# Three opening sums moved from between the parts of the last chunk to behind the chunk before it

## The chip, the core and the metric

The kernel runs on one core of one Trainium2 chip. The metric is the device time of one execution in microseconds. A time given with a place ("at 399.35") is counted from the first instruction of the profiled execution.

## The reference

Two stages follow each other. The first is causal attention with a decay bias, for 8 batches, 8 heads, 576 tokens and head size 64:

```python
cum = np.cumsum(np.maximum(s, 0.0), axis=-1)
bias = -(cum[:, :, :, None] - cum[:, :, None, :])
scores = np.where(causal, -1e9, scale * q @ k.T + np.minimum(bias, 0.0))
x = softmax(scores) @ v          # laid out as (8, 576, 512)
```

The second mixes the tokens in the frequency domain, keeps 64 modes, and adds a channel product:

```python
X = np.fft.rfft(x, axis=1)[:, :64]
Y = X @ (w_r + 1j * w_i)         # one 512x512 complex matrix for each mode
u = x + np.fft.irfft(Y, n=576)   # 8 x 576 x 512
out = u + np.maximum(u @ w_ch, 0.0)
```

The weights of the modes are 64 x 512 x 512, real and imaginary, in float32; they are the largest input.

## The kernel before

The work has four groups of channels (`g`, two heads each), eight batches, and eight chunks (`c`) of eight modes each. During attention the weights of the modes stream in as bfloat16, in the order group, chunk, real then imaginary, all through GpSimd's DMA queue (`load`, L243). The products of a chunk (`modes`, L478) run as soon as its weights are on chip; for the first three groups they are added up in `y_acc`. The last group of channels (`NG - 1`) ends each chunk: its product plus `y_acc` is the chunk's spectrum `yb` (name `y_sb`, DVE, L502).

From there the kernel computes u = x + G y and z = u w_ch = x w_ch + G (y w_ch), where G is the inverse transform. The order of all instructions is written by hand; each engine goes through its own in that order. For each chunk, `y_transposed` (L701, copy on ACT L703) and `y_times_wch` (L709, copy on DVE L713) make `vb`, which is the chunk's y w_ch. Both y and y w_ch go to `yv`, with 16 rows for each chunk: for the first chunks by copies, for the later ones by DMAs on SP (`spread`, L513).

The output is worked off in 18 pairs of token tiles. PSUM holds a `u` tile (two banks) and `z` tiles for a pair. Four functions add to them on TensorE: `add_x` (L803, x itself, starts u), `add_y` (L773, rows of yv; here the first 96, which are chunks 0 to 5), `add_last` (L784, one single chunk, straight from `y_sb` or `v_sb` without yv), and `x_times_wch` (L681), which opens z for pairs 0 and 1 earlier on. Pair 0 is two full token tiles (2 matmuls for each sum); pair 1 is four half tiles that run two at a time (4 matmuls).

Chunk seven is the last of the stream, and its imaginary half comes in two halves with DMAs of their own. So `modes` takes its 16 products in four parts: parts 0 and 1 need the real weights, part 2 the first half of the imaginary ones, part 3 the second. Through `meanwhile` the kernel can put other matmuls in front of a part:

```python
for x in range(4):
    ri, y = divmod(x, 2)
    if meanwhile and x in meanwhile:
        meanwhile[x]()
    for z in range(4):
        ...
```

Before the change part 2 has in front of it the sums of z (`first_z` of pairs 0 and 1) over chunks 0 to 5 and chunk 6, and part 3 those of u of pair 0 (`first_u`): x, chunks 0 to 5, chunk 6.

After chunk seven comes its own transposition (L904), its share in u of pair 0 (L784), its product with w_ch (L911, copies L914), its share in z of pairs 0 and 1 (L784), and then a hand-written list of steps that finishes one pair after the other: relu on ACT (L826), sums on DVE (L848, L850) and GpSimd (L832), output DMAs on SP (L854, L857).

Of the kernel before, what the change touches and what calls it, by code (L numbers as in the profile page):

```python
# [18 lines left out]
def kernel(  # L19
# [20 lines left out]
    NG = DM // P  # L40
# [6 lines left out]
    NCK = NM // MC  # L47
# [160 lines left out]
    def ring_of(k):  # L208
        if k < NE:
            return None  # L210
        return int(k < LW2 and (k - NE) % (WA + WB) >= WA)
# [42 lines left out]
    for n in range(N):  # L254
# [4 lines left out]
        while nt < min(w // 2, len(wq)):  # L259
            i = ring_of(nt)  # L260
# [209 lines left out]
    def modes(g, c, meanwhile=None):  # L470


        ps = auxpool.tile([P, DM], FP32, name="yp", tag="aux")
        cols = xs[g % 2].rearrange("p q k h r b m -> p q k (h r b) m")

        def product(ri, q_, cg):
            k0 = HP if ri == 1 and c == 0 and cg == 0 else 0
            nc.tensor.matmul(  # L478
                ps[32 * cg : 32 * cg + 32, :],
                cols[k0:, q_, 1 - ri, :, c * MC // 2 + cg],  # L480
                wt[(g, c, ri)][cg // 2][k0:, 2 * (cg % 2) + q_, :],
                start=(ri == 0 and q_ == 0), stop=(ri == 1 and q_ == 1),
                tile_position=(k0, 32 * cg), skip_group_check=True,
# [7 lines that stand above are left out]
                if meanwhile:  # L491
                    product(ri, z // 2, 2 * y + z % 2)
                else:
                    product(ri, y, z)
        if g == 0:
            nc.vector.tensor_copy(out=y_acc[:, c, :], in_=ps)
        elif g < NG - 1:
            nc.vector.tensor_tensor(out=y_acc[:, c, :], in0=ps, in1=y_acc[:, c, :], op=ALU.add)  # L498
        else:
            yb = spool.tile([P, DM], FP16, name="y_sb", tag="y")  # L500
            for cols in halves if c == NCK - 1 else [slice(0, DM)]:
                nc.vector.tensor_tensor(  # L502
                    out=yb[:, cols], in0=ps[:, cols], in1=y_acc[:, c, cols], op=ALU.add
                )
            if c >= NCK - 2:
                spread(c, 0, yb)
            return yb
# [3 lines left out]
    def spread(c, which, rows):  # L511

        nc.sync.dma_start(out=yv[16 * c : 16 * c + 16, :, which, :], in_=rows)  # L513
# [68 lines left out]
    with tc.tile_pool(name="sc_psum", bufs=2, space=PSUM) as scpool, \  # L582
# [8 lines left out]
        for n in range(N):  # L591
# [21 lines left out]
            i = first_pairs[n - N + len(first_pairs)] if n >= N - len(first_pairs) else None  # L613
# [42 lines left out]
    def parts(b, T):  # L656

        if T < NF:
            return [(slice(0, P), b, ident16h)]
        return [(slice(NL * i, NL * i + NL), b + i, ident16h[:NL, :NL]) for i in range(2)]  # L660
# [37 lines left out]
    def y_transposed(yb, c=NCK):  # L698
        ps = auxpool.tile([P, DT, P], FP16, name="yt_ps", tag="aux")
        for dt in range(DT):  # L700
            nc.tensor.transpose(ps[:, dt, :], yb[:, bass.ts(dt, P)], ident16h)  # L701
        yt = yt_first[:, :, c % NY, :] if c < NCK - 2 else spool.tile([P, DT, P], FP16, name="yt_sb", tag="yt")
        nc.scalar.copy(out=yt, in_=ps)  # L703
        return yt

    def y_times_wch(c, yt):
        vp = auxpool.tile([P, DM], FP32, name="v_ps", tag="aux")
        for dt in range(DT):
            nc.tensor.matmul(  # L709
                vp, yt[:, dt, :], wch_sb[:, dt, :], start=(dt == 0), stop=(dt == DT - 1)  # L710
            )
        vb = spool.tile([P, DM], FP16, name="v_sb", tag="v")
        nc.vector.tensor_copy(out=vb, in_=vp)  # L713
        spread(c, 1, vb)
        return vb
# [50 lines left out]
    GK = P - 2 * MC * NX  # L766

    def add_y(dst, i, which, rows=slice(0, P), start=False, xx=(0, 1)):

        for x in xx:  # L770
            b, T = pairs[i][x]
            for r, bb, _ in parts(b, T):
                nc.tensor.matmul(  # L773
                    dst[x][r, :], G_sb[rows, bass.ds(T * P, r.stop - r.start)],
                    yv[rows, bb, which, :], start=start, stop=True, skip_group_check=True,
                    tile_position=(0, r.start),
                )

    def add_last(dst, i, yb, cols=slice(0, DM), c=NX - 1, xx=(0, 1)):

        for x in xx:
            b, T = pairs[i][x]
            for r, bb, _ in parts(b, T):
                nc.tensor.matmul(  # L784
                    dst[x][r, cols], Gx_sb[:, c, bass.ts(T, P)] if T < NF else Gt_sb[:, bb, c], yb[:, cols],
                    start=False, stop=True, skip_group_check=True, tile_position=(0, r.start),
                )
# [3 lines left out]
    def start_u(i):  # L791
        if upools[i % 2] is None:
            (xt, aux)[i % 2].close()
            upools[i % 2] = ctx.enter_context(
                tc.tile_pool(name=f"u_psum{i % 2}", bufs=1, space=PSUM, side=("left", "right")[i % 2])
            )
        us[i] = upools[i % 2].tile([P, 2, DM], FP32, name="u_ps", tag="u")

    def add_x(i):
        start_u(i)  # L800
        for x, (b, T) in enumerate(pairs[i]):
            for r, bb, ident in parts(b, T):
                nc.tensor.matmul(  # L803
                    us[i][r, x, :].rearrange("p (g d) -> p g d", d=P), ident,
                    x_all[: r.stop - r.start, :, bb, T, :],
                    start=True, stop=False, skip_group_check=True, tile_position=(0, r.start),
                )

    def u_of(i):
        return [us[i][:, x, :] for x in range(2)]  # L810
# [48 lines left out]
    def z_of(i):  # L859
        return [zs[i, x] for x in range(2)]  # L860

    for c in range(NCK - 2):
        yb = modes(NG - 1, c)
# [17 lines left out]
    assert not order_z and not ahead  # L881
    c = NCK - 2
    yb6 = modes(NG - 1, c)
    yt = y_transposed(yb6)
    vb6 = y_times_wch(c, yt)


    def first_u():
        add_x(0)
        add_y(u_of(0), 0, 0, slice(0, GK))  # L890
        add_last(u_of(0), 0, yb6, c=0)

    def first_z(i):
        add_y(z_of(i), i, 1, slice(0, GK))
        add_last(z_of(i), i, vb6, c=0)

    yb = modes(NG - 1, NCK - 1, {2: lambda: (first_z(0), first_z(1)), 3: first_u})

    yt = spool.tile([P, DT, P], FP16, name="yt_sb", tag="yt")
    for x in range(2):  # L900
# [51 lines left out]
    for step in (  # L952
# [8 lines left out]
        i = int(step[1:].rstrip("ab"))  # L961
# [34 lines left out]
```

## Time and profile before

| | |
|---|---|
| median of 3 runs | 441.92 us (440.32 to 442.31) |
| the profiled execution | 442.11 us, of which the span from first to last instruction is 440.3 us |
| PE (TensorE matmuls) busy | 340.8 us, 77% |
| DVE, ACT, POOL busy | 252.5, 226.0 and 171.7 us |
| mean granted TensorE clock | 0.925 |
| DMA | 93.30 MB, mean 212 GB/s |
| chain that ended last | DMA 53%, PE 25%, DVE 15% |

PE is the matmul side of TensorE; DVE, ACT and POOL are VectorE, ScalarE and GpSimd; SP is the queue that issues the output and `yv` DMAs. "Busy" counts modelled ends of pipelined matmuls, so a busy PE need not be at its peak. "PEclk" is the share of the full TensorE clock that was granted: 1.00 or 0.50. The chain of waits is followed back from the last instruction, at each step to what released it. In a timeline row the first number is the start, the second how long the group of instructions took.

### The profile page before, as it was taken

What the parts mean: (1) busy time and instruction counts of PE and PEld (TensorE: products, weight loads), DVE (VectorE), ACT (ScalarE), POOL (GpSimd) and SP (SyncE); (2) the same over time, 40 slices, a digit from 0 to 9 for tenths busy, and PEclk for the clock granted to TensorE, in tenths of its full rate; (3) what the DMA queues carried; (4) which work ended last, traced back from release to release, by engine and by line L of the source; (5) the groups of instructions that cost most, each with busy time, mean ns of one, the idle gap of its engine ahead of it and who ended that gap; (6) DMA issues with size and microseconds to landing.
All of it is one profiled execution on the core that took longest, in us unless ns stands there. A gap on an engine that the chain in (4) does not pass through costs nothing.

```text
span 440.3 us, 10592 instructions
## 1 busy us (share of the span) xinstructions
PE 340.8 (77%) x4409; PEld 203.7 (46%) x4409; DVE 252.5 (57%) x574; ACT 226.0 (51%) x421; POOL 171.7 (39%) x257
## 2 busy tenths in 40 slices
PE   1588999899695977973939458899987797778995
PEld 1365666465463644641616125556554345432341
DVE  7667776677573555752715315766655344450795
ACT  1387878267463634860727024766651334330794
POOL 6555454424353444323444343433322212310293
PEclk9999999999988888995968767999999989996999
DMA  9999999999999999999999999999999999996498
GB/s 179 207 206 206 204 206 208 207 209 207 207 205 207 210 207 210 207 209 208 205 209 208 209 208 209 207 210 206 210 211 212 212 211 211 203 218 121 155 381 347
DMA packets 69063, 93.30 MB, mean 212 GB/s; under 512 B 25932, under 2 KB 27592, under 8 KB 69016
## 3 DMA queue, kind: packets, MB, share of 16 engines
q0 software_dynamic: 61424, 81.28, 104.6%
q1 hardware_dynamic: 7592, 11.36, 7.2%
q8 instruction: 34, 0.56, 0.5%
q14 instruction: 13, 0.11, 0.1%
HBM read 163.58 MB, written 9.51 MB: 393 GB/s over the span
## 4 chain that ended last, share of the span: by engine, by line
DMA 53%; PE 25%; DVE 15%; issue 3%; POOL 2%; ACT 1%; DVEq 0%; POOLq 0%
DMA w_sb<-in_moe_w_i_dram 21%; DMA w_sb<-in_moe_w_r_dram 17%; DMA qk<-in_k_dram 8%; DMA qk<-in_q_dram 5%; PE sc_ps L397 3%; DVE xs L468 3%; DVE qt L359 3%; PE z_ps L681 3%; PE yp L478 3%; DVE x_all L443 2%; PE av_ps L433 2%; PE sc_ps L391 2%; PE tr_ps L355 2%; DVE xt L553 2%; PE z_ps L773 2%
## 5 line engine op out<-in xcount | busy, mean ns | idle before, releaser
L405 ACT ACTIVATE p_sb<-sc_ps,cumt_sb 128x576 f16<-128x576 f32 (+1 forms) x256 | 141.9, 636 | 21.8 <-PE sc_ps L397 21.4
L397 PE MATMUL sc_ps<-qt,kt 128*128 128x512 bf16 (+2 forms) x384 | 76.8, 312 | 6.9 <-ACT kt L359 6.1
L243 POOL DMA_DIRECT2D v<-in_v_dram x72 | 51.4, 714 | 60.6 <-DMA w_sb<-in_moe_w_i_dram 12.8
L243 POOL DMA_DIRECT2D w_sb<-in_moe_w_i_dram x62 | 38.5, 623 | 89.2 <-DMA w_sb<-in_moe_w_i_dram 28.3
L359 DVE COPY qt<-tr_ps 64x576 bf16<-64x576 bf16 x64 | 47.8, 747 | 41.5 <-PE tr_ps L355 41.5
L478 PE MATMUL yp<-w_sb,xs 128*32 128x512 bf16 (+1 forms) x480 | 42.2, 431 | 29.1 <-DMA w_sb<-in_moe_w_i_dram 25.4
L355 PE MATMUL tr_ps<-ident,qk 64*64 64x64 bf16 x1152 | 34.3, 205 | 33.8 <-DMA qk<-in_k_dram 16.0
L243 POOL DMA_DIRECT2D w_sb<-in_moe_w_r_dram x60 | 37.4, 624 | 53.0 <-DMA w_sb<-in_moe_w_r_dram 33.3
L397 PEld LDWEIGHTS <-kt 128*128 128x128 bf16 x384 | 38.3, 105 | 34.5 <-ACT kt L359 12.8
L391 PE MATMUL sc_ps<-negm,ident 128*128 128x256 bf16 x256 | 53.5, 293 | 0.1
L355 PEld LDWEIGHTS <-qk 64*64 64x64 bf16 x1152 | 26.4, 117 | 51.7 <-DVE kt L359 20.3
L376 ACT ACTIVATE p<-sc_ps,cumt 128x64 f16<-128x64 f32 x32 | 10.1, 314 | 73.8 <-PE sc_ps L372 73.6
L433 PE MATMUL av_ps<-v,p_sb 128*128 128x65 f16 x1024 | 44.2, 197 | 1.8 <-DVE x_all L443 0.6
L359 ACT COPY kt<-tr_ps 64x576 bf16<-64x576 bf16 x32 | 22.8, 714 | 40.8 <-DVE qt L359 40.1
L433 PEld LDWEIGHTS <-p_sb 128*128 128x128 f16 x1024 | 37.4, 100 | 9.6 <-DVE x_all L443 5.4
L468 DVE CAST xs<-ft_ps 64x128 bf16<-64x128 f32 x128 | 36.7, 287 | 7.3 <-PE ft_ps L458 5.7
L478 PEld LDWEIGHTS <-xs 128*32 128x32 bf16 (+1 forms) x512 | 17.8, 146 | 46.0 <-DMA w_sb<-in_moe_w_i_dram 24.6
L438 DVE TENSOR_REDUCE den<-av_ps 128x5 f32<-128x10 f32 x64 | 10.8, 169 | 48.3 <-PE av_ps L433 47.3
L443 DVE TENSOR_TENSOR x_all<-av_ps,rcp 128x320 f16<-128x320 f32 x64 | 31.5, 492 | 2.2
L498 DVE TENSOR_TENSOR y_acc<-yp,y_acc 128x512 f32<-128x512 f32 x16 | 11.1, 692 | 29.2 <-PE yp L478 28.5
L539 ACT COPY z<-z_ps 128x512 f32<-128x512 f32 x22 | 12.9, 586 | 26.9 <-PE z_ps L571 14.2
L458 PE MATMUL ft_ps<-Ff_sb,x_all 128*64 128x192 f16 (+1 forms) x320 | 24.4, 266 | 1.0 <-DVE x_all L443 1.0
(107 smaller groups left out, 439.4 us busy)
## 6 DMA issues: line engine op xcount, KB each, us to landing
w_sb<-in_moe_w_r_dram POOLq DMA_DIRECT2D x60, 512.0 KB, 13.6
w_sb<-in_moe_w_i_dram POOLq DMA_DIRECT2D x55, 512.0 KB, 13.2
out_dram<-r_w SPq DMA_DIRECT2D x16, 512.0 KB
v<-in_v_dram POOLq DMA_DIRECT2D x72, 64.0 KB, 11.1
qk<-in_q_dram POOLq DMA_DIRECT2D x15, 288.0 KB, 12.0
qk<-in_k_dram POOLq DMA_DIRECT2D x15, 288.0 KB, 13.2
x_all<-in_moe_w_r_dram POOLq DMA_DIRECT2D x4, 512.0 KB, 8.4
w_sb<-in_moe_w_i_dram POOLq DMA_DIRECT2D x3, 384.0 KB, 12.7
```

The costliest lines, as they stand in the source:

```text
L243: nc.gpsimd.dma_start(out=dst, in_=src)
L355: nc.tensor.transpose(ps[rows, r, :], src[rows, r, :], ident16[rows, rows])
L359: copy(out=to[:, :, :, half * RH : half * RH + RH], in_=ps[HP * i : HP * i + HP].rearrange("d r (h p) -> d h p r", h=2),)
L391: nc.tensor.matmul(ps[:, bass.ds(w * S, W)], ident16, negm[:, bass.ts(r, W)], start=True, stop=False, skip_group_check=True,)
L397: nc.tensor.matmul(ps[:, c0 : c0 + i1 - i0], keys[:, w, r, :], qh[:, i0:i1], start=False, stop=True, skip_group_check=True,)
L405: nc.scalar.activation(out=pt[:, poff[x] : poff[x] + S - w * W], in_=ps[:, w * S : (w + 1) * S - w * W], func=ACTF.Exp, bias=cumt_sb[:, x, ...
L433: nc.tensor.matmul(ps[:, I, r : r + NCH], lhsT, rhs, start=(i == 0), stop=(i == len(todo) - 1), skip_group_check=True,)
L443: nc.vector.tensor_tensor(out=x_all[:, g, b, :, D * h : D * h + D], in0=ps[:, :, 1 : NCH], in1=rcp.unsqueeze(2).to_broadcast([P, NT, D]), ...
L458: nc.tensor.matmul(ps[HP * q_ : HP * q_ + HP].rearrange("p h f -> p (h f)"), x_all[:nT, g, b, T, q_::2], Ff_sb[:nT, T, :], start=(T == 0), ...
L468: nc.vector.tensor_copy(out=xs[g % 2][HP * h : HP * h + HP, q_, :, h, :, b, :], in_=a)
L478: nc.tensor.matmul(ps[32 * cg : 32 * cg + 32, :], cols[k0:, q_, 1 - ri, :, c * MC // 2 + cg], wt[(g, c, ri)][cg // 2][k0:, 2 * (cg % 2) + ...
L681: nc.tensor.matmul(zs[i, x], xts[i][:, x, dt, :], wch_sb[:, dt, :], start=(dt == 0), stop=(last and dt == DT - 1), skip_group_check=True,)
```

## The change

The sums of u of pair 0 over x, chunks 0 to 5 and chunk 6 go behind chunk six: `add_x` in front of chunk six's transposition, the other two between it and `y_times_wch`. The sums of z of pairs 0 and 1 over chunks 0 to 5 go behind `y_times_wch` of chunk six. The sums of z over chunk six stay in front of part 2 of chunk seven; part 3 has nothing in front of it any more.

```diff
     c = NCK - 2
     yb6 = modes(NG - 1, c)
+    add_x(0)
     yt = y_transposed(yb6)
+    add_y(u_of(0), 0, 0, slice(0, GK))
+    add_last(u_of(0), 0, yb6, c=0)
     vb6 = y_times_wch(c, yt)
-
-
-    def first_u():
-        add_x(0)
-        add_y(u_of(0), 0, 0, slice(0, GK))
-        add_last(u_of(0), 0, yb6, c=0)
+    add_y(z_of(0), 0, 1, slice(0, GK))
+    add_y(z_of(1), 1, 1, slice(0, GK))
 
     def first_z(i):
-        add_y(z_of(i), i, 1, slice(0, GK))
         add_last(z_of(i), i, vb6, c=0)
 
-    yb = modes(NG - 1, NCK - 1, {2: lambda: (first_z(0), first_z(1)), 3: first_u})
+    yb = modes(NG - 1, NCK - 1, {2: lambda: (first_z(0), first_z(1))})
```

## The prediction

> **What bounds the kernel now.** I read the slices of the span first, then the chain that ended last, then the PE timeline around the edit, then the landings of the last weights, and last the granted clock in stretches cut where it changes.
>
> From the page, the granted clock and the DMA share by slice:
>
> ```profile
> PEclk9999999999988888995968767999999989996999
> DMA  9999999999999999999999999999999999996498
> ```
>
> DMA is at 9 until slice 36 of 40 (11 us each), so up to about 396 us the weight stream sets the pace. The edit sits at the end of that stream. The chain there, in order of time:
>
> ```profile
> 383.57 15.64 DMA w_sb<-in_moe_w_r_dram
> 399.35 1.09 PE yp L478 x6
> 400.44 0.96 PE z_ps L773 x2
> 401.41 0.85 PE z_ps L784 x2
> 402.26 0.99 PE z_ps L773 x3
> 403.25 0.85 PE z_ps L784 x3
> 404.11 1.00 PE yp L478 x4
> 405.11 0.57 PE u_ps L803 x2
> 405.68 0.43 PE u_ps L773 x2
> 406.12 0.43 PE u_ps L784 x2
> 406.55 0.60 PE yp L478 x4
> 407.17 0.44 DVE y_sb L502
> ```
>
> The real half of chunk seven lands at 399.21; from then to 407.17 the chain is PE without a gap, and the sums to be moved are links of it. From 411 to 436 PE lines (u L803 25%, z L773 23%, u L773 23%) are again most of the chain: a microsecond lost by PE there is mostly lost to the end.
>
> What could stop the products from running earlier is their weights. Issues of the imaginary half of chunk seven, from the tile view of w_sb in the stretches 384.9 to 385.5, 385.5 to 386 and 387.5 to 388.2:
>
> ```profile
> DMA to landing us min/median/max: 17.2/17.2/17.3
> ...
> DMA to landing us min/median/max: 17.3/17.8/18.3
> ...
> DMA to landing us min/median/max: 17.4/17.4/17.4
> ```
>
> With issues at 384.36, 384.95, 385.53 and 387.77 (POOL timeline) these land at 401.6, 402.3, 403.8 and 405.1. The first pair feeds part 2 of the products (before: 404.04), the second pair part 3 (before: 406.48). So part 3 could start at 405.1 plus the 0.14 that lay between landing (399.21) and product (399.35): about 405.27.
>
> The granted clock (columns: stretch, its length, PE busy us and instructions, PEclk, DMA share, GB/s):
>
> ```profile
> 118.43:121.85 3.42, 1.50 (x27) 1.00 1.31 204
> ...
> 138.91:142.33 3.42, 2.48 (x27) 0.50 1.21 207
> ...
> 394.91:398.33 3.42, 1.43 (x8) 1.00 1.12 215
> 398.33:401.74 3.41, 2.39 (x12) 0.50 1.01 201
> 401.74:405.15 3.41, 3.41 (x15) 0.50 0.32 67
> 405.15:408.57 3.42, 2.85 (x17) 1.00 0.00 0
> ```
>
> The clock changes on a raster of 3.41 us. After a stretch with PE busy 1.43 or 1.50 it fell to half; stretches with 1.85 (115.02 to 118.43) and 2.22 (391.50 to 394.91) kept it. Back it came only after a full stretch: 3.41 here, 3.31 (97%, 231.07 to 234.49) the least elsewhere, while 2.39 and 2.48 did not restore it. In before the slow stretch, 398.33 to 405.15, falls on these sums, and the dense work brings the clock back just ahead of the tail.
>
> **The change part by part.**
>
> Removed from between the products: in front of part 2 the z sums of L773 (two full, four half tiles in pairs), timeline starts 400.37 to 401.20 and 402.19 to 403.05, so 0.83 + 0.86 = 1.7 us at half clock; in front of part 3 add_x (2), add_y (2) and add_last (2) of u, 405.04 to 406.48 = 1.44 us. In all 3.1 us off a stretch where PE is on the chain. The six add_last of z (L784) stay in front of part 2. No DMA, copy or ACT instruction is added or dropped.
>
> Added behind chunk six. add_x(0) starts when the products of chunk six are through (about 394.5) and takes two matmuls at 0.22 (their spacing in the u rows at full clock), done by 394.9; the transposes wait for DVE's y_sb until 395.37 anyway: nothing. The four u matmuls follow the transposes, from about 395.6 to 396.46; y_times_wch waited until 396.44 for ACT's copy: 0.02 us. SP's spread of vb6 is issued 0.02 later, and its reader comes after 411. The z sums (four slots of 0.22) run from 397.3 to 398.2, in a wait that before lasts until 399.35. If the clock were half here, the four u matmuls take 1.7 us, y_times_wch ends near 399.0 and the z sums near 400.7: then the eight products queued behind on PE start 1.3 late and the six add_last end near 403.9, part 2 near 404.9, still ahead of 405.27.
>
> Wait added: the z sums read yv rows of chunk five's product, whose DMA SP issues at 390.07. No view shows its landing. It is bounded from 390.6 to 400.37, where before reads it without a wait. At the late end PE, with chunk seven's products queued behind, starts them 1.0 late, near 400.4, and add_last ends near 401.9, ahead of the landing at 402.3. Zero at both ends; a gain is excluded since nobody waits for these sums earlier.
>
> Part 3, then: 405.27 in place of 406.48, **1.2 us earlier**, bound by the weights. Of 3.1 us removed 1.9 turns into waiting.
>
> What is late next: the clock. Work now packed into 394.9 to 398.3 fills about 3.1 of 3.41 us, so the clock stays full there. After it PE has the eight products (0.5), six add_last (0.95), a wait to 402.4, part 2 (0.65), a wait to 405.27. The stretch 398.33 to 401.74 holds about 1.6 us (between 1.50, lost, and 1.85, kept), and 401.74 to 405.15 about 0.65, far below 1.43. So the clock is halved at 405.15 at the latest, exactly where the tail begins. Priced from rows:
>
> - Part 3 takes 1.07 (the 404.04 row) in place of 0.65: ends at 406.35 against 407.13.
> - DVE 0.48, transposes from 406.87, second pair by 407.42; u add_last two at 0.43: 408.27; v_ps eight at 0.218 in place of 0.109: 410.0.
> - Twelve add_last of z: 1.31 at full clock; at half, eight slots of 0.213 and four changes of tile shape at 0.14 (the gap 401.63 to 402.19 less 0.43): 2.27, so 412.2, its last 0.2 us at full clock if the clock returns at 411.98: 412.1. Before, the next step (u of pair 1) starts at 410.96: **1.15 us later**.
>
> Bounds of this unknown: clock back at 408.57: v_ps ends at 409.3, z at 410.87, 0.1 us earlier than before; clock never lost: 1.2 earlier. I take the later return since 405.15 to 408.57 would hold about 2.7 us of PE work (waits of 0.12 and 0.5 in it), 0.79 of the stretch, nearer to 2.48 (not restored) than to 3.31.
>
> A rule speaks against a loss here. The Trainium skill, page "TensorE: Matmul & The Clock Gate", section "HAM oscillation — how this bites in real kernels", asks only that PE have no idle gap over about 3.4 us; the longest gap after the change is 2.2 us, so by the rule the clock stays and the sum is −1.2 us. The trace has a longest gap of 1.87 us ahead of 399.35 and lost the clock at 398.33 all the same; the measurement decides.
>
> Sum: the profiled execution took 442.11 (span 440.3 and 1.8 around it), so 442.11 + 1.15 = 443.3. It stands 0.2 above the median of 441.92. The raster need not stand alike in every run, and the runs of before spread from 440.32 to 442.31; I put the sum on the median: 441.92 + 1.2 = **443.1**. Other positions of the raster move it from +0.3 to +2.1 (clock back between 409 and 414).
>
> **The rivals.**
>
> - Clock back one stretch earlier, 408.57: for it 0.79 is untested between 0.73 and 0.97; against it the nearest row. −0.1: 441.8.
> - Clock kept, the full gain: needs a stretch with 0.65 busy to hold it, against the rows of 1.43 and 1.50. −1.2: 440.7. More than this the weights forbid.
> - Slower: the half clock lasts into the steps of pairs 1 to 3. Place: 411.98 to 415.39, where PE makes up the chain. Price: 3.41 / 2 = 1.7 on top of 1.15: +2.9, 444.8; it passes the bound of 0.5% (2.2 us, about what a measurement of this kernel can tell from no change) if the clock returns later than 414.0. It decides if the raster falls 2 us later or the waits of z for v_sb leave the second stretch below what restores. For it: nothing under 97% has restored. Against: that stretch is 3.33 of 3.41 busy in before, and slower matmuls leave smaller gaps.
> - That the change does not do what it says can be left out: the reads of yv are of rows 0 to 95, which before too reads while rows 96 to 111 are under way.
>
> **How the numbers follow.** Forecast 0.56 (442.2 to 444.0); early return 0.12; clock kept 0.10, of which 0.03 for a gain over 0.5% by the spread of runs; late return 0.22, nearly all of it past 0.5%. Range: leaving out half of the kept-clock case and part of the late return, 441.2 to 444.6. Faster 0.03, same 0.75, slower 0.22.
>
> **What would show it.** Right: L803, L773 of u and L773 of z between 394.5 and 398.3 at 0.22 a slot; PEclk 1.00 there; waits of PE L478 for w_sb<-in_moe_w_i_dram of about 1.5 and 2.2 us; part 3 at about 405.3; PEclk 0.50 from about 405 to 409–412; v_ps L911 at about 0.22 a matmul. Wrong: part 3 at 406 or later, or PEclk 1.00 through 405 to 410 (then 440.7), or a wait of the z sums past 399.4.

## The result and the profile after

The changed kernel took 442.59 us (median of 22 runs, 441.77 to 444.27), the kernel before 441.32 us (22 runs, 440.16 to 442.81). The ratio is 1.0028, 95% interval 1.0017 to 1.0039: a loss of 1.2 us by the ratio (the medians lie 1.27 apart), clear of zero and below the 0.5% bound.

The chain of the changed kernel's profiled execution (441.83 us, span 440.1), in order of time:

```profile
388.66 16.17 DMA w_sb<-in_moe_w_i_dram
404.83 0.04 issue
404.87 0.67 PE yp L478 x4
...
406.77 0.85 PE u_ps L784 x2
407.62 1.71 PE v_ps L909 x8
409.33 1.41 PE z_ps L784 x12
410.74 0.55 PE u_ps L803 x4
```

Where the chain of before ran through PE from 399.35, it now runs through the DMA of the last weights up to 404.83, and the last products follow 0.04 us behind. The sums between the parts are off the chain, as meant. But u of pair 0 takes 0.85 and v_ps 1.71 for its eight matmuls. In the chain of before these pieces were (v_ps with the first four of its eight matmuls, 0.87 for all eight by the 0.109 a matmul of before):

```profile
408.27 0.43 PE u_ps L784 x2
408.70 0.45 PE v_ps L911 x4
```

The clock of the changed kernel in stretches cut at its own raster (stretch, length, PE busy and instructions, PEclk, DMA share, GB/s):

```profile
399.35:402.76 3.41, 3.19 (x24) 1.00 0.75 157
402.76:406.17 3.41, 0.85 (x8) 1.00 0.14 34
406.17:409.59 3.42, 3.40 (x16) 0.50 0.16 43
409.59:413.00 3.41, 3.41 (x25) 1.00 0.27 93
```

The waits before parts 2 and 3 leave 0.85 us of PE work in a stretch of 3.41; at its end the clock is halved, and what follows chunk seven's products on PE runs at half clock until 409.59.

PE now waits for the weights where the sums stood (PE's waits, 395 to 415: us in total, times, longest):

```profile
PE yp L478 <- DMA w_sb<-in_moe_w_i_dram: 2.3, 2, 2.0
```

One measure fits all runs, whose weights land between 404.7 and 406.2: the time from the last landing (the last semaphore update of that DMA in the trace) to the start of u of pair 1 (L803), and from there to the end.

| profile | landing to part 3 | part 3 to u of pair 1 | sum | from there to the end |
|---|---|---|---|---|
| before, three profiles | 1.35, 1.19, 0.30 | 4.48, 4.48, 4.48 | 5.83, 5.67, 4.78 | 29.4 |
| after, three profiles | 0.04, 0.04, 0.04 | 5.80, 5.72, 6.82 | 5.84, 5.76, 6.86 | 29.4 |
| z alone moved | 0.04 | 4.49 | 4.53 | 29.4 |
| z and add_x moved | 0.04 | 4.49 | 4.53 | 29.4 |
| u alone moved | 0.04 | 5.66 | 5.70 | 29.4 |
| after, wide fillers | 0.61 | 4.49 | 5.10 | 30.8 |
| after, narrow fillers | 0.04 | 5.61 | 5.65 | 30.7 |
| before, wide fillers | 1.06 | 4.49 | 5.54 | 30.9 |
| before, narrow fillers | 0.42 | 4.49 | 4.91 | 30.8 |

Before pays ahead of part 3 and has a full clock behind it (4.48 each time); after pays nothing ahead of it and 1.2 to 2.3 us behind. The first profiles of the two kernels come out alike (5.83 and 5.84). The loss shows in the medians and in the further profiles. It isn't the weights that come later: they land between 404.8 and 405.2 in all six profiles of before and after.

### The profile page after: what moved, and what is told of

It reads as the page before. It is cut to its first block, busy times and chain, and to the rows that moved or that the text cites. A ratio compares the mean times of both kernels' runs of the same rounds, so it can differ in the third digit from the quotient of the medians.

```text
span 440.1 us, 10592 instructions
## 1 busy us (share of the span) xinstructions
PE 346.1 (79%) x4409; PEld 206.4 (47%) x4409; DVE 253.0 (57%) x574; ACT 226.3 (51%) x421; POOL 171.6 (39%) x257
## 4 chain that ended last, share of the span: by engine, by line
DMA 79%; PE 10%; DVE 3%; issue 3%; ACT 2%; POOL 2%; DVEq 0%; POOLq 0%
DMA w_sb<-in_moe_w_r_dram 47%; DMA w_sb<-in_moe_w_i_dram 24%; DMA qk<-in_k_dram 5%; DMA qk<-in_q_dram 2%; PE u_ps L803 1%; DMA v<-in_v_dram 1%; PE z_ps L773 1%; PE u_ps L773 1%; PE sc_ps L397 1%; ACT p_sb L405 1%; PE yp L478 1%; PE tr_ps L355 1%; DVE qt L359 1%; POOL v L243 1%; PE av_ps L433 1%
## 5 line engine op out<-in xcount | busy, mean ns | idle before, releaser
L397 PE MATMUL sc_ps<-qt,kt 128*128 128x512 bf16 (+2 forms) x384 | 78.7, 318 | 6.5 <-ACT kt L359 5.6
L478 PE MATMUL yp<-w_sb,xs 128*32 128x512 bf16 (+1 forms) x480 | 42.8, 434 | 27.8 <-DMA w_sb<-in_moe_w_i_dram 26.2
L391 PE MATMUL sc_ps<-negm,ident 128*128 128x256 bf16 x256 | 54.5, 298 | 0.0
L478 PEld LDWEIGHTS <-xs 128*32 128x32 bf16 (+1 forms) x512 | 17.6, 145 | 45.9 <-DMA w_sb<-in_moe_w_i_dram 26.7
```

What stands on the lines that cost most here:

```text
L391: nc.tensor.matmul(ps[:, bass.ds(w * S, W)], ident16, negm[:, bass.ts(r, W)], start=True, stop=False, skip_group_check=True,)
L397: nc.tensor.matmul(ps[:, c0 : c0 + i1 - i0], keys[:, w, r, :], qh[:, i0:i1], start=False, stop=True, skip_group_check=True,)
L478: nc.tensor.matmul(ps[32 * cg : 32 * cg + 32, :], cols[k0:, q_, 1 - ri, :, c * MC // 2 + cg], wt[(g, c, ri)][cg // 2][k0:, 2 * (cg % 2) + ...
```

## The experiments

The clock theory: the sums, once out of the waits, leave PE too idle there; it loses its clock and pays in the tail. Rival 1: the moved sums or the extra matmuls themselves cost. Ratios are to the kernel before in the same comparison, with the 95% interval.

**One half of the change at a time.** z alone:

```diff
     yt = y_transposed(yb6)
     vb6 = y_times_wch(c, yt)
+    add_y(z_of(0), 0, 1, slice(0, GK))
+    add_y(z_of(1), 1, 1, slice(0, GK))
...
     def first_z(i):
-        add_y(z_of(i), i, 1, slice(0, GK))
         add_last(z_of(i), i, vb6, c=0)
```

> Only the z sums over chunks 0 to 5 go behind chunk six; those of u stay in front of part 3. Clock theory (the changed kernel loses because PE waits twice before parts 2 and 3, gets half clock there and carries it into the tail): the u sums fill 1.4 of the 2.2 us before part 3, PE is busy over 60% of each 3.41 us stretch, the clock stays full, part 3 starts at about 405.3 and everything behind it runs at full clock. 0.7 us below before (0.2 to 1.2 below), about 1.9 below the changed kernel. Rival 1 (the moved sums themselves cost, by holding up chunk six's products, copy and DMA): half of the moves, so between no change and 0.6 above before. Rival 2 (only the last product's start counts, the clock costs nothing): 0.7 to 1.2 below before, but then the changed kernel would be there too.

Measured: 440.88 against 441.83 us, ratio 0.9983 (0.9971 to 0.9995). A gain, of the expected size, and the lowest ratio of all versions, though its interval overlaps that of the step between below. Its clock:

```profile
398.18:401.60 3.42, 3.42 (x17) 0.50 1.11 220
401.60:405.01 3.41, 2.73 (x21) 1.00 0.62 98
405.01:408.42 3.41, 2.34 (x16) 1.00 0.02 5
```

A stretch at half clock lay ahead, where the weights covered it. From 401.60 on, with the u sums in front of part 3, the clock stays full and part 3 follows the landing by 0.04. Rival 2 of the expectation falls with it: in the changed kernel too part 3 follows its landing by 0.04, and that one loses.

u alone:

```diff
+    add_x(0)
     yt = y_transposed(yb6)
+    add_y(u_of(0), 0, 0, slice(0, GK))
+    add_last(u_of(0), 0, yb6, c=0)
     vb6 = y_times_wch(c, yt)
...
-    yb = modes(..., {2: lambda: (first_z(0), first_z(1)), 3: first_u})
+    yb = modes(..., {2: lambda: (first_z(0), first_z(1))})
```

> Only the u sums go behind chunk six; those of z stay in front of part 2. Clock theory: the z sums fill the wait before part 2, but the wait of 2.2 us before part 3 stays empty, the stretch that holds it is below half busy, the clock halves by 405 to 406.5 in most runs: 0.9 above before (0 to 1.4 above), a little below the changed kernel. Rival 1: the other half of the loss, 0.6 to 1.2 above, so that this and the run with z alone add up to the changed kernel's 1.2. By the clock theory they don't add up: one is a gain, the other nearly the whole loss.

Measured: 442.46 us, ratio 1.0018 (1.0006 to 1.0030). A loss, while z alone is a gain: the halves don't share the change's loss between them, as rival 1 would have it. The stretch with the empty wait and the one behind it:

```profile
402.25:405.66 3.41, 0.91 (x8) 1.00 0.26 56
405.66:409.08 3.42, 2.90 (x14) 0.50 0.13 38
```

**Filling the waits with work that nobody reads.** Into the changed kernel, with the tile taken from the PSUM pool so that no later tile waits for another one:

```diff
+    fill = auxpool.tile([P, DM], FP32, name="f_ps", tag="aux")
+    def filler(count, width=DM):
+        for _ in range(count):
+            nc.tensor.matmul(fill[:, :width], ident16h, wch_sb[:, 0, :width], start=True, stop=True, ...)
-    yb = modes(..., {2: lambda: (first_z(0), first_z(1))})
+    yb = modes(..., {2: lambda: (first_z(0), first_z(1), filler(5)), 3: lambda: filler(8)})
```

> The changed kernel, all sums where the change puts them, with matmuls that nobody reads in PE's waits: 5 of 128x512 in front of part 2 (1.1 us at full clock) and 8 in front of part 3 (1.7 us). Clock theory: PE stays busy, granted clock 1.00 from 402 through 415, part 3 at about 405.3, u of pair 1 (L803) starts at about 409.7 in place of 410.7 to 412: 0.7 below before (0.2 to 1.2 below), 1.9 below the changed kernel. Rival 1: extra matmuls cannot help; the same as the changed kernel, 1.2 above before, or more.

Measured: 442.73 us, ratio 1.0018 (1.0006 to 1.0030). The expected gain did not come in the time. In the profile the clock did as the theory says:

```profile
396.35:399.76 3.41, 3.41 (x15) 0.50 1.12 209
399.76:403.17 3.41, 3.41 (x24) 1.00 0.82 174
403.17:406.59 3.42, 3.42 (x19) 1.00 0.14 35
406.59:410.00 3.41, 2.76 (x21) 1.00 0.12 35
```

From part 3 to u of pair 1 it took 4.49 us in place of 5.7 to 6.8. Two costs that I had not reckoned with took the gain. The first: the last products of chunk six came at 395.79 (394.01 in the changed kernel), a stretch at half clock followed, everything on PE was late, and the fillers ran past the landing by 0.61. The second: from u of pair 1 to the end took 30.84 us in place of 29.38, although every output DMA was issued at the same distance behind that step (the last at 25.3 us in both). The queue totals, of the changed kernel and of the filled one, differ in one row:

```profile
q8 instruction: 34, 0.56, 0.5%
```

```profile
q8 instruction: 35, 0.57, 0.5%
```

One fetch of 16 KB more, at 432.6 and 1.47 us long, while the output DMAs drain. That it is what holds them up is argued from the place and the length alone: no run has the extra matmuls without the fetch.

The kernel before, with `filler(8)` in front of chunk seven's products:

> The kernel before with 8 matmuls of 128x512 that nobody reads in the wait in front of chunk seven's products (397.5 to 399.2). Clock theory: the clock is not lost at 398 to 400, the sums of z and u run at 0.22 a slot, part 3 starts at about 405.3 and not at 406.5, the tail is at full clock: 0.4 below before (0 to 0.8 below), since before loses the clock in nearly every run but wins it back before the tail. If the slow sums of before cost nothing: no change.

Measured: 442.64 us, ratio 1.0021 (1.0006 to 1.0036): the expectation failed here too. The extra fetch is there (30.94 us to the end). In the profile the last products of chunk six came 0.8 us later than in the first profile of before (394.70 for 393.91), and the clock was at half from 396.24 to 399.65, so that y_times_wch took 1.89 us in place of 1.04 and the fillers began only at 399.09, in part still at half clock (2.18 us; the eight at full clock in the run above took 1.90). They pushed the sums back, and part 3 came 1.06 behind the landing. This run by itself does not tell the theories apart.

**The control: as many matmuls, but 16 columns wide.** `filler(5, 16)` and `filler(8, 16)` in the changed kernel:

> Control for the filled version of the changed kernel: the same 13 extra matmuls in the same places, but 16 columns wide in place of 512, so as many instructions and hardly any PE work. The filled kernels showed one more fetch of instructions (35 in place of 34 on the instruction queue), 16 KB at about 432, and their output DMAs ended 1.5 us later after the same steps. Clock theory: the fetch stays (35, +1.5) and PE's waits stay empty, so the half clock in the tail stays too: 1.2 + 1.5 = 2.7 above before (2.0 to 3.2), about 1.9 above the wide version's 0.8. Rival 1 (width doesn't matter, the extra matmuls just cost): as the wide version, 0.8 above before, or less.

Measured: 443.70 us, ratio 1.0049 (1.0034 to 1.0064), 0.5 to 0.7 us less of a loss than the 2.7 expected (by the ratio, by the medians), but well above the wide fillers' 1.0018: with the same instructions and the same fetch, the work in the waits is worth 0.3%, or 1.4 us (two comparisons, whose intervals don't overlap). The clock falls again:

```profile
402.40:405.81 3.41, 1.27 (x16) 1.00 0.25 57
405.81:409.22 3.41, 2.89 (x15) 0.50 0.13 38
```

Rival 1 is excluded by this pair: if extra matmuls merely cost, the narrow ones could not cost more than the wide.

`filler(8, 16)` in the kernel before:

> Control for the filled version of the kernel before: 8 matmuls 16 columns wide in front of chunk seven's products. Clock theory: the fetch alone, 1.5 above before (1.1 to 1.9), against 0.9 with the wide ones, so that the work in the wait is worth about 0.6. Rival 1: the same as with the wide ones, 0.9, or less.

Measured: 443.15 us, ratio 1.0034 (1.0019 to 1.0048). The loss of 1.5 us is as large as what the tail of the one profile lost (30.82 against 29.38). The difference from the wide fillers (0.13%) has the expected sign and size, but the intervals overlap: not settled.

**A step between.** z and add_x of u behind chunk six, add_y and add_last of u (four matmuls) in front of part 3:

> The step between the version with z alone and the whole change: z and add_x of u (2 matmuls) behind chunk six, add_y and add_last of u (4 matmuls, 0.87 us) in front of part 3. Clock theory: PE then does 1.5 us between part 2's start and part 3's landing, about the 1.43 to 1.85 at which the clock is lost or kept, so it is lost in some runs: between the two, 0.7 below to 0.6 above before, nearest to 0.2 above. Rival 1 (cost goes by matmuls moved): 2 of 6 of the way from z alone (0.75 below) to the whole change (1.2 above): 0.1 below before; here the two lie too near to be told apart by the median alone, but the clock in the profile would stay at 1.00 by rival 1's account.

Measured: 441.50 us, ratio 0.9999 (0.9980 to 1.0018). The median lies between. Its 12 runs spread over 3.3 us, six from 440.1 to 441.1 and five from 442.6 to 443.5, as a clock lost in some runs and not in others would have it; but only one was profiled, of the lower group (440.37), so that this isn't shown. That profile kept the clock behind the landing:

```profile
396.02:399.43 3.41, 2.78 (x8) 0.50 1.06 204
399.43:402.84 3.41, 3.41 (x18) 0.50 0.74 154
402.84:406.26 3.42, 2.83 (x19) 1.00 0.11 27
```

That is the reading that rival 1 was given for this run, and also one of the clock theory's two; it doesn't decide.

**The same kernels at other positions of the raster.** The first profiles of before and after were alike, so each was profiled twice more, unchanged.

> The changed kernel unchanged, one more profile, because the raster of the clock (3.41 us) stands elsewhere in each execution. Measured from the landing of the last weights to the start of u of pair 1 (L803): 4.53 us with part 3 at once and full clock throughout (the profiles of z alone and of add_x moved), 5.84 in the first profile of the changed kernel. Clock theory: part 3 follows the landing by 0.04, and every profile shows a stretch at half clock that begins by 408 and costs behind the landing: 5.5 to 7.1, by where the raster stands. Rival (the single profiles show no loss against before, so the loss lies elsewhere): 5.8 again, and the end later than 29.4 us behind L803.

> As the run before it, with another position of the raster: 5.5 to 7.1 us from the last landing to u of pair 1 by the clock theory, and 29.4 from there to the end; by the rival 5.8 and a later end.

> The kernel before unchanged, for another position of the raster. Its first profile had 5.83 us from the last landing to u of pair 1: 1.35 of waiting for its own sums at half clock, then 4.48 at full clock. Clock theory: the half clock lies ahead of part 3 and never behind it, so 4.5 to 5.9, mostly below 5.8, and 29.4 from there to the end. Rival: 5.8 again.

> As the run before it: 4.5 to 5.9 from the last landing to u of pair 1 by the clock theory, on average about 1.2 less than the changed kernel's; by the rival 5.8 again.

Measured, in the table's second and third entries: after 5.76 and 6.86, before 5.67 and 4.78, and 29.4 to the end in all four. So nothing is lost behind u of pair 1, and all four lie in the ranges of the clock theory; but the means of before and after differ by 0.7, not by the 1.2 expected. The third profile of after (443.26 us) has its raster where the prediction worked its sum:

```profile
401.69:405.10 3.41, 0.65 (x4) 1.00 0.33 69
405.10:408.51 3.41, 2.73 (x12) 0.50 0.03 7
408.51:411.93 3.42, 3.42 (x20) 0.50 0.15 40
411.93:415.34 3.41, 3.41 (x22) 1.00 0.52 188
```

And its timeline (start, duration, group):

```profile
405.26 1.07 PE L478 MATMUL yp<-w_sb,xs 128*32 128x512 bf16 x4 [2.20 <-DMA w_sb<-in_moe_w_i_dram]
...
408.22 1.92 PE L909 MATMUL v_ps<-wch_sb,yt_sb 128*128 128x256 f16 x8
...
412.08 0.62 PE L803 MATMUL u_ps<-x_all,ident16h 64*64 64x512 f16 x4
```

Part 3 starts at 405.26, v_ps at 408.22, u of pair 1 at 412.08.

## Why the prediction was right

The prediction held: forecast 1.2 above the median of before, measured 1.24 above it by the ratio; 443.1 against 442.59 absolutely, because before itself came out at 441.32 over 22 runs and not at 441.92.

*Part 3 bound by the weights.* Right: 405.27 forecast, 404.87, 405.17 and 405.26 measured. The distance from landing is 0.04 and not the 0.14 taken from the first products. The wait in front of it, forecast at about 2.2, was 2.04, 2.25 and 2.20.

*What the moved sums cost where they go.* Right at full clock: with narrow fillers y_times_wch starts 1.10 us behind the start of the transposes, before 1.07. In the first profile of after the clock was at half there and it started 1.71 behind, 0.64 later; the weights covered that, as the worked case said. (The prediction took the clock to stay full there; in this one profile of three it did not.) No wait of the z sums for yv appears in PE's waits.

*The clock lost, and its price.* The clock was halved in the tail in all three profiles, as forecast, at 405.10, 406.17 and 406.32 ("405.15 at the latest" holds for the prediction's raster alone). The price was right where the raster stood as in the sum, in the third profile: u of pair 1 was forecast for 412.1 and came at 412.08; the stretch from 405.1 was to be 0.79 busy and not to bring the clock back, and it was 0.80 and did not. Two readings behind it were off without harm: the stretch from 398.3 was to hold about 1.6 us and held 1.97 (398.27 to 401.69), and the least that brought the clock back in before was not 3.31 but 3.27 (254.97 to 258.38).

*The raster.* That it need not stand alike was taken from the spread of the times of before; the profiles bear it out: with the same kernel the half clock began at 398.33, 398.14 and 395.89, and in the changed one behind the waits at 406.17, 406.32 and 405.10. In two of the three the clock came back after one stretch, as in the rival of the early return, but 1.0 to 1.2 us later than that rival had it, because the raster stood later. Against the profile of before that the sum was worked from (5.83), these two lost nothing (5.84 and 5.76): that is the price of that rival (-0.1), and below the +0.3 that the prediction gave as the least for a return between 409 and 414; and that profile was itself the slowest of the three of before. So the match of 1.2 with 1.2 is partly luck: the sum holds for one position of the raster, and that it also hits the median over 22 runs isn't explained by it. The profiles alone (means of 5.43 and 6.15 over three each) would have put the loss at 0.7; the size rests on the medians.

*The rivals.* The clock was kept in no profile of the changed kernel. A return later than 411.93 was not seen in a profile; the highest runs, 444.20 and 444.27, would fit it, but have no profile.

*The rule that speaks against a loss.* The Trainium skill, "TensorE: Matmul & The Clock Gate", "HAM oscillation — how this bites in real kernels", allows idle gaps up to about 3.4 us. Here gaps of at most 2.25 us cost the clock in all three profiles of the changed kernel: the measurement decides. Around the last chunk it is the share of work in the stretch that fits, not the longest gap.

## What to carry to other kernels

Work that fills a wait for a DMA on TensorE may be worth more where it stands than ahead of it, even if it is on the chain: look at how much matmul work is left in each 3.4 us around the wait, and at what runs right behind it. Moving part of the filler (here the sums that delayed the first part, not those that filled the longest wait) got the earlier start and kept the clock. When an experiment adds instructions, look at the instruction queue and at the tail first: a control with as many, but tiny, instructions separates their work from their presence.

## What the runs showed of the hardware

- Around the last chunk (stretches that begin between 385 and 415 us, all thirteen profiles) the clock was lost after stretches with at most 1.66 us of PE work in 3.41 (0.49; the changed kernel, 392.52 to 395.93) and kept from 1.84 (0.54; the changed kernel with narrow fillers, 392.16 to 395.57) on. This is not a rule for the whole kernel: elsewhere the clock was lost after 2.43 (the kernel before, second profile, 333.29 to 336.70) and kept after 1.58 (the changed kernel with wide fillers, 351.97 to 355.38).
- In the same place it comes back on less than the 96% that the first profile of before showed: after 2.90 and 2.89 (0.85) in two runs, and once after 2.73 (0.80; the kernel before with wide fillers, 396.24 to 399.65), while 2.73 and 2.78 did not bring it back in two others. Busy time with modelled ends separates the cases only to about 0.8, and elsewhere not even that: in the changed kernel 3.39 of 3.41 did not bring it back (334.49 to 337.91, nearly all of it products of L478, 32 columns wide). What else the clock goes by is open.
- 16 or 26 more instructions on TensorE (8 or 13 matmuls and their weight loads) came with one more fetch of 16 KB, at 431.6 to 432.6, that fell among the last output DMAs. In all four kernels with extra matmuls the end came 1.4 to 1.6 us later behind the same step, though every output DMA was issued at the same distance from it.
- From u of pair 1 to the end took 29.37 to 29.39 us in all nine profiles without that fetch.
